# A fused attention, MLP and soft-MoE kernel: the denominator's reciprocal by way of DRAM instead of TensorE, K earlier, and the outputs' products in groups of four between second-layer products

## The chip, the cores and the metric

One NeuronCore of a Trainium2 chip runs the whole program. The time is device microseconds of one execution. Before the change three runs took 1055.14 to 1058.01 us, median 1057.03.

## What is computed

Inputs are q, k, v of 8 batches x 8 heads x 576 rows x 64, all fp32 (the weights w_in and w_out come as float64 words).

```python
def phi(x):                                  # 64 -> 128 -> 256 features
    proj = x @ w_phi
    proj = proj - max(abs(proj), axis=-1)
    return concat([exp(proj), exp(-proj)])
kv  = sum_s phi(k) v ;  z = sum_s phi(k)
x   = (phi(q) @ kv) / (phi(q) @ z + 1e-6)    # -> [4608, 512]
h   = x @ w_in                               # 512 -> 2048
g   = max(h, 0) + alpha * min(h, 0)
x   = g @ w_out                              # 2048 -> 512
logits = x @ phi                             # 512 -> 32 slots
d   = softmax(logits, over the 4608 tokens)
slot_input = d.T @ x                         # 32 x 512, 4 slots for each of 8 experts
slot_out[e] = max(slot_input[e] @ w1[e], 0) @ w2[e]
c   = softmax(logits, over the 32 slots)
out = c @ slot_out                           # [4608, 512]
```

## The kernel before, in words

Tokens go in 12 blocks of 384 (n = 0 to 11), the 2048 columns of w_in in 16 chunks (c). A pair (n, c) is a *slot* of the program; everything is registered for a slot with `at`, and a scheduler then sets each engine's order by slot and readiness. After the slots of blocks 4 and 7 stand five extra *virtual* steps each, in which two deferred blocks (0 and 1), whose g went to DRAM, are read back and finished. w_out is folded with phi at the start, so that g gives logits directly; x after w_out is never formed for all tokens, only the 32 sums over tokens (`pS`).

- `k_pair` (32 of them, one per batch and head pair): K's features (`pk`, `kp`), then kv and z (`pkv`, `pt`, `kv_t`, `zt`). `q_pair` (4 per block): load `qraw`, product `pq`, GpSimd's reduction, `qe`, then numerators `num` (L435) and denominators `den` (L442).
- `q_finish` (L453 on): ACT adds 1e-6 (`rd`), TensorE sums the two signs (`densum`, L460), DVE takes the reciprocal (L464), ACT and DVE split it into two float32r halves (`rhl`), TensorE spreads each head's row over 64 partitions by a selecting matrix (`sel`, L477 and L478, two products per p, eight per block), DVE multiplies the numerators by it (L484), ACT and DVE split x into `xhi` and `xlo`.
- `gemm` (L505): twelve float32r products of 128x128 by 128x384 per slot into `ph` (two banks); `leaky` makes g (`gT`); `turn_g` transposes it into `gb` and forms logits `pl` every fourth chunk; `softmax` keeps a running maximum, and `gather` and `add` accumulate `pS` into `acc`.
- The weights w1 and w2 and a copy of the folded w_out come in 144 pieces of 256 KB, prefetched into every buffer that falls free (`fetch`), 100 of them before the tail's own work, 44 when their buffers have been read (L686).
- Tail, after the last `gemm`: last softmax and `pS`, `pg`/`px` (slot sums times w_out), `psi`, `pe` (first layer), `pth` (TensorE transposes of h), `pso` (second layer, L819), `prp`, then `po` (L836): the outputs, each half of 256 columns in 36 products, copied by ACT and DVE into one of three 512 KB buffers `os` and written by 18 DMAs (L842). `pc` are transposes of the combine weights. `spin` issues products on an identity that nobody reads, so that TensorE stays busy.

SP issues every DMA, in its own order: a DMA that waits for its buffer holds up those behind it.

Of the kernel before, what the change touches and what calls it, by code (L numbers as in the profile page):

```python
# [28 lines left out]
TB = BT // 128  # L29
NT = T // 128  # L30
E = 8
# [3 lines left out]
KVB = 6  # L35
# [8 lines left out]
SPIN = [5, 3, 13, 6]  # L44

F64_LEAST = struct.unpack("<f", struct.pack("<I", 0x38100000))[0]
# [15 lines left out]
def attention_prelu_softmoe(ctx: ExitStack, tc, qT, kT, v, wphi, w_in, w_out, alpha, phi, w1, w2, out):  # L62
# [10 lines left out]
    gT_d = dram.tile([NDEF, NC, 128, BT], F32, name="gT_d")  # L73

# [27 lines left out]
    def spin(count, before):  # L102
        turn = bank("spin", ps_d)
# [28 lines left out]
    eps_den = const.tile([128, 1], F32, name="eps_den")  # L132
    densum = att.tile([128, 128], F32, name="densum")
    densel = xp.tile([128, NP, 128], F32R, tag="densel", name="densel")

    wpr = sm.tile([128, NC, NSL], F32, tag="wpr", name="wpr")
    acc = const.tile([128, 4, 512], F32, name="acc")
# [5 lines left out]
    def setup_a():  # L143
        nc.vector.memset(ones, 1.0)
        nc.vector.memset(eps_den, 0.0)
        nc.vector.memset(eps_den[0:32], 1e-6)
        nc.vector.memset(eps_den[64:96], 1e-6)

    def setup_b():
# [8 lines left out]
        for p in range(NP):  # L158
            for j in range(2):
                a, b = 64 * j + p, 64 * j + 32 + p  # L160
                r = 32 * p + 16 * j
                nc.vector.tensor_tensor(
                    out=densum[:, r:r + 16], in0=ident[:, a:a + 1].to_broadcast([128, 16]),
                    in1=ident[:, b:b + 1].to_broadcast([128, 16]), op=ALU.add)
                nc.vector.tensor_copy(densel[:, p, 64 * j:64 * j + 64], ident[:, r:r + 1].to_broadcast([128, 64]))

    sched = {}

# [14 lines left out]
    def conv(slot, src, use):  # L183
# [21 lines left out]
        def second():  # L205
# [3 lines left out]
            nc.vector.tensor_tensor(out=w, in0=m, in1=st["sign"], op=ALU.mult)  # L209
# [172 lines left out]
    def q_pair(slot, n, p, late=0):  # L382
# [44 lines left out]
        def attend():  # L427
# [25 lines left out]
    def q_finish(slot, n):  # L453
        st = q_st[n]

        def sums():
            rd = st["rd"] = sm.tile([128, BT], F32, tag="dT", name="rd")
            nc.scalar.activation(rd, st["den"][:, 0:BT], AF.Identity, bias=eps_den)
            ps = st["ps"] = bank("densum")
            nc.tensor.matmul(ps[:, 0:BT], densum, rd, start=True, stop=True)  # L460
# [28 lines left out]
        at(slot, "pe", sums)  # L489
        at(slot, "post", recip)  # L490
        at(slot + 1, "pre", split)
        for p in range(NP):
            at(slot + 1, "post", spread(p))
            at(slot + 1, "post", scale(p))
# [15 lines left out]
    def leaky(n, c, h):  # L510
        gT = gT_t[n, c] = sm.tile([128, 512], F32, tag="gT", name="gT", bufs=5)[:, 0:BT]
        if n < NDEF or (c % 2 == 0 and n < NB - 1):
            nc.scalar.activation(gT, h, AF.Relu, scale=-1.0)  # L513
            nc.scalar.activation(h, h, AF.Relu)  # L514
            nc.vector.scalar_tensor_tensor(out=gT, in0=gT, scalar=alpha_neg[:, c:c + 1], in1=h, op0=ALU.mult, op1=ALU.add)  # L515
        else:
            nc.vector.tensor_scalar(out=gT, in0=h, scalar1=0.0, scalar2=alpha_sb[:, c:c + 1], op0=ALU.min, op1=ALU.mult)  # L517
            nc.vector.scalar_tensor_tensor(out=gT, in0=h, scalar=0.0, in1=gT, op0=ALU.max, op1=ALU.add)
# [3 lines left out]
    def reload(n, c):  # L522
        gT4 = attk.tile([128, 4, BT], F32, tag=f"vg{c // 4 % 2}", name="gT4")
# [374 lines left out]
```

## Time and profile before

| | |
|---|---|
| median of three runs | 1057.03 us (1055.14 to 1058.01) |
| the profiled execution's own time | 1057.16 us |
| its span, first to last instruction | 1055.4 us |
| TensorE busy | 984.1 us (93%), mean granted clock 0.964 of full |
| DVE, ACT busy | 773.8 us (73%), 469.8 us (45%) |
| moved by DMA | 110.6 MB |

The profile has one line per group of instructions: engine, line of the kernel, result<-operands, shape, count, busy time, mean of one, and the idle time of that engine ahead of them with what ended it. A window view gives each engine's busy time in a stretch, with the granted TensorE clock (1.00 is 2.4 GHz, 0.5 is 1.2 GHz) and the DMA engines' share.

### The profile page before, as it was taken

The page shows a single profiled execution, that of the slowest core. Times are in us where ns is not written, and L with a number is a line of the kernel's source. Part 1 is how long each engine was busy: PE and PEld are TensorE (multiplying, and loading weights), DVE is VectorE, ACT ScalarE, POOL GpSimd, SP SyncE. Part 2 cuts the span into 40 slices and gives each one's busy share as a digit, 9 for nine tenths or more (in the row PEclk, how much of TensorE's full clock was granted, in tenths as well). Part 3 has the DMA queues.
Part 4 walks back from the last instruction along what each step waited for, and adds up shares of the span by engine and source line. Part 5 has one row for each costly group of instructions (what it writes and reads, how often), then busy time and mean ns, then how long its engine had stood idle before and what let it go on. Part 6 is the DMA issues. An engine that isn't in the chain of part 4 may idle for free.

```text
span 1055.4 us, 21864 instructions
## 1 busy us (share of the span) xinstructions
PE 984.1 (93%) x9038; PEld 685.2 (65%) x9038; DVE 773.8 (73%) x1552; ACT 469.8 (45%) x908; POOL 149.2 (14%) x88
## 2 busy tenths in 40 slices
PE   3787998998999999999999999999999999998994
PEld 1445776774676776676666776767667767787353
DVE  3999989879767578587878687687888486874133
ACT  3876867776444245144235344343334343200133
POOL 2201214121111212121112111121112221000000
PEclk7898999998999999999999999999999999999995
DMA  5343653653010111010401111110401200769879
GB/s 199 120 141 125 193 188 114 225 178 100 9 31 31 39 31 38 20 51 19 163 10 38 32 39 31 31 38 19 160 19 46 96 8 2 249 226 327 261 235 309
DMA packets 71986, 110.60 MB, mean 105 GB/s; under 512 B 7248, under 2 KB 47312, under 8 KB 71888
## 3 DMA queue, kind: packets, MB, share of 16 engines
q1 hardware_dynamic: 71888, 109.22, 32.0%
q8 instruction: 71, 1.16, 0.4%
q14 instruction: 27, 0.22, 0.1%
HBM read 89.27 MB, written 19.92 MB: 103 GB/s over the span
## 4 chain that ended last, share of the span: by engine, by line
PE 71%; DVE 3%; DMA 2%; ACT 1%; issue 1%; DVEq 0%; ACTq 0%; SPq 0%
PE ph L505 34%; PE num L435 5%; PE pS L602 5%; PE pkv L333 5%; PE pl L540 4%; PE den L442 3%; PE pq L403 3%; PE pk L289 2%; DMA out_dram<-os 2%; PE pso L819 1%; PE pe L782 1%; PE sel L477 1%; PE pt L355 1%; PE pr L558 1%; PE densum L460 1%; PE pkv L339 1%
## 5 line engine op out<-in xcount | busy, mean ns | idle before, releaser
L505 PE MATMUL ph<-xhi,w 128*128 128x384 f32 x1536 | 435.2, 351 | 6.5 <-DVE gT L515 4.4
L505 PEld LDWEIGHTS ph<-xhi,w 128*128 128x128 f32 x1536 | 279.0, 189 | 76.8 <-issue 41.5
L505 PE MATMUL ph<-xlo,w 128*128 128x384 f32 x768 | 255.1, 340 | 0.0
L415 POOL PARTITION_ALL_REDUCE mb<-pj x48 | 140.4, 2928 | 553.0 <-ACT pj L409 450.1
L505 PEld LDWEIGHTS ph<-xlo,w 128*128 128x128 f32 x768 | 143.6, 188 | 12.6 <-issue 6.1
L515 DVE SCALAR_TENSOR_TENSOR gT<-gT,alpha_neg,ph 128x384 f32<-128x384 f32 x104 | 62.9, 605 | 77.3 <-ACT ph L514 76.5
L532 DVE STREAM_TRANSPOSE gb<-gT 128x384 f32<-128x384 f32 x192 | 105.6, 566 | 5.7 <-DMA gT<-gT_d 1.9
L513 ACT ACTIVATE gT<-ph 128x384 f32<-128x384 f32 x104 | 50.8, 489 | 114.8 <-PE ph L505 114.0
L425 ACT ACTIVATE qe<-pj 128x768 f32<-128x768 f32 x92 | 73.9, 839 | 59.5 <-DVE pj L419 56.2
L517 DVE TENSOR_SCALAR gT<-ph,alpha_sb 128x384 f32<-128x384 f32 x88 | 53.8, 613 | 46.2 <-PE ph L505 45.8
L333 PE MATMUL pkv<-kp,vt 128*64 128x256 f32 (+1 forms) x640 | 85.0, 400 | 1.1 <-DVE wpr L250 1.1
L435 PE MATMUL num<-qe,kv 128*64 128x192 f32 (+1 forms) x496 | 70.9, 417 | 0.0
L283 ACT ACTIVATE kp<-kp 128x512 f32<-128x512 f32 (+1 forms) x80 | 46.8, 586 | 51.6 <-DVE kp L282 51.1
L333 PEld LDWEIGHTS pkv<-kp,vt 128*64 128x64 f32 (+1 forms) x640 | 41.3, 140 | 39.4 <-issue 17.1
L280 DVE TENSOR_REDUCE mx<-pk 128x4 f32<-128x512 f32 (+1 forms) x80 | 50.2, 627 | 11.4 <-PE pk L289 9.7
L602 PE MATMUL pS<-gb,d 32*32 32x256 f32 x2304 | 55.0, 385 | 0.3 <-DVE logits L594 0.2
L403 PE MATMUL pq<-qraw,wp 64*128 64x384 f32 x192 | 48.9, 562 | 6.7 <-DMA qraw<-in_qT_dram 4.1
L446 ACT COPY num<-num 128x384 f32<-128x384 f32 x48 | 22.8, 475 | 67.1 <-PE num L435 64.2
L409 ACT COPY pj<-pq 128x768 f32<-128x768 f32 x44 | 35.2, 799 | 36.3 <-PE pq L403 36.3
L419 DVE TENSOR_TENSOR pj<-pj,mb 128x768 f32<-128x768 f32 x48 | 46.6, 971 | 6.0 <-POOL mb L415 6.0
L282 DVE TENSOR_TENSOR kp<-pk,mx 128x512 f32<-128x512 f32 (+1 forms) x80 | 50.2, 627 | 0.8 <-PE pkv L333 0.2
L514 ACT ACTIVATE ph<-ph 128x384 f32<-128x384 f32 x104 | 50.6, 487 | 0.0
(191 smaller groups left out, 1345.6 us busy)
## 6 DMA issues: line engine op xcount, KB each, us to landing
w<-in_w_dram SPq DMA_DIRECT2D x58, 256.0 KB, 5.7
qraw<-in_qT_dram SPq DMA_DIRECT2D x48, 192.0 KB, 2.4
out_dram<-os SPq DMA_DIRECT2D x18, 512.0 KB, 3.7
raw<-in_w_in_dram SPq DMA_DIRECT2D x16, 512.0 KB, 3.6
raw<-in_w_out_dram SPq DMA_DIRECT2D x16, 512.0 KB, 4.2
gT_d<-gT SPq DMA_DIRECT2D x32, 192.0 KB, 2.0
gT<-gT_d SPq DMA_DIRECT2D x8, 768.0 KB, 5.2
pf<-in_w_dram SPq DMA_DIRECT2D x21, 256.0 KB, 6.0
```

Source lines behind the costliest of these rows:

```text
L333: return lambda: nc.tensor.matmul(pkv[64 * j:64 * j + 64, 0:256], vt[:, 64 * j:64 * j + 64], feats(t, j).rearrange("p s f -> p (s f)"), st ...
L403: lambda j=j, sl=slice(64 * j, 64 * j + 64): nc.tensor.matmul(pq[j][:, 0:BT], wp[sl], st["qraw"][sl], start=True, stop=True)
L415: nc.gpsimd.partition_all_reduce(mb, pj, 128, bass_isa.ReduceOp.absmax)
L425: nc.scalar.activation(st["e", s], pj, AF.Exp, scale=(1.0, -1.0)[s])
L435: lambda s=s, j=j: nc.tensor.matmul(num[64 * j:64 * j + 64, o:o + w], kvs[:, s, 64 * j:64 * j + 64], st["e", s][:, j, o:o + w], start=(s = ...
L505: gemm_last[0] = nc.tensor.matmul(h, (w_in_hi, w_in_lo)[a][c][:, 128 * k:128 * k + 128], (xhi, xlo)[b][:, k, :], start=(i == 0), stop=(i = ...
L513: nc.scalar.activation(gT, h, AF.Relu, scale=-1.0)
L514: nc.scalar.activation(h, h, AF.Relu)
L515: nc.vector.scalar_tensor_tensor(out=gT, in0=gT, scalar=alpha_neg[:, c:c + 1], in1=h, op0=ALU.mult, op1=ALU.add)
L517: nc.vector.tensor_scalar(out=gT, in0=h, scalar1=0.0, scalar2=alpha_sb[:, c:c + 1], op0=ALU.min, op1=ALU.mult)
L532: nc.vector.transpose(out=gb[n, c // 8][:, c % 8, :], in_=gT)
L602: lambda j=j, i=i, h=h: nc.tensor.matmul(pS[i][32 * (j % 4):32 * (j % 4) + 32, 256 * h:256 * h + 256], st["d"][32 * i:32 * i + 32, 32 * j: ...
```

## The change

1. **Reciprocal.** `den` is accumulated for both signs and both halves of a block's tokens in four column groups, so it needs no sum and holds 192 columns. DVE adds 1e-6 and takes the reciprocal of 128x192, SP writes it to DRAM (`rc_d`, two DMAs), and reads it back broadcast over 64 partitions (`bc`, two DMAs). Six slots on, DVE multiplies the numerators by it from SBUF (`divide`, held behind that slot's last marked DVE instruction). The set-up of the summing and selecting matrices, `rd` on ACT, `densum`, `rhl` and `sel` are gone. `q_finish` stands at slot 16(n-1)+7 (was +11), the multiplications at +13 (was +12).
2. **K.** Pairs 8 and on come up to eight slots sooner, with eight kv buffers (six); `q_pair`s stand three slots apart (four).
3. **Read-back of g** in tiles of two chunks: three buffers of two and the ring of `gT`, instead of two buffers of four.
4. **Tail.** `acc` in four tiles; for the last block TensorE adds the old sums (`carry`) and the copies are shared by ACT and DVE; first-layer results are masked and transposed by DVE (no `pth`); w2 pieces take rows 64 KiB apart for the partitions, in runs of 1 KB (2 KB apart before); combine weights stay transposed, so an output group is four products on 32 rows each (L859), without `pc`. Second-layer groups of the second half stand between the first nine output groups, with `spin`. Nine `os` buffers (three).

```diff
-SPIN = [5, 3, 13, 6]
+SPIN = [5, 3, 8, 3, 8, 5, 5, 5, 3]
...
-            for b, o, w in segments(n):
-                kvs, zt = kv_t[NP * b + p]
+            for s in (1, 0):
                 together([
-                    lambda g=g: nc.tensor.matmul(
-                        den[32 * g:32 * g + 32, o:o + w], zt[:, g, :], st["e", g % 2][:, g // 2, o:o + w],
-                        start=(p == 0 and o == 0), stop=(p == NP - 1 and o + w == BT))
-                    for g in (3, 1, 2, 0)])
+                    lambda j=j, h=h, zt=kv_t[NP * ((n * BT + h * HB) // S) + p][1]: nc.tensor.matmul(
+                        den[64 * j + 32 * h:64 * j + 32 * h + 32, 0:HB], zt[:, 2 * j + s, :],
+                        st["e", s][:, j, HB * h:HB * h + HB],
+                        start=(p == 0 and s == 1), stop=(p == NP - 1 and s == 0))
+                    for j in (1, 0) for h in (1, 0)])
...
         def recip():
-            rc = st["rc"] = sm.tile([128, BT], F32, tag="dT", name="rc")
-            nc.vector.reciprocal(out=rc, in_=st["ps"][:, 0:BT])
...
+            nc.vector.tensor_scalar(out=rd, in0=st["den"][:, 0:HB], scalar1=1e-6, scalar2=None, op0=ALU.add)
+            nc.vector.reciprocal(out=rd, in_=rd)
+            for j in range(2):
+                nc.sync.dma_start(rc_d[n % 2][j].rearrange("p h t -> h p t"), rd[64 * j:64 * j + 64])
+        def widen():
+            bc = st["bc"] = xp.tile([128, NP, BT], F32, tag="bc", name="bc")
+            for j in range(2):
+                nc.sync.dma_start(
+                    bc[64 * j:64 * j + 64], rc_d[n % 2][j, 0:NP].rearrange("p h t -> p (h t)").unsqueeze(0).to_broadcast([64, NP, BT]))
...
+                ins = nc.vector.tensor_tensor(out=xs, in0=st["bc"][:, p, :], in1=xs, op=ALU.mult).ins
+                tc.add_manual_dep(ins, mark[max(k for k in mark if k <= slot + 6)].name, nosync, reason="behind the load")
...
+        at(slot + 1, "pre", widen)
         for p in range(NP):
-            at(slot + 1, "post", spread(p))
-            at(slot + 1, "post", scale(p))
+            at(slot + 6, "post", divide(p))
+        for p in range(NP):
+            at(slot + 6, "post", scale(p))
...
-        k_pair(int(-40 + 2.5 * i) if i < 4 else int(-20 + 6 * (i - 4)) if i < 8 else 6 * i + -42, i)
+        k_pair(int(-40 + 2.5 * i) if i < 4 else int(-20 + 6 * (i - 4)) if i < 8 else 6 * i - 42 - min(i - 8, 8), i)
...
-                src = w2[e, 256 * c:256 * c + 256, 256 * dh:256 * dh + 256].rearrange("(c p) d -> p c d", p=128)
+                src = w2[4 * eg:4 * eg + 4].rearrange("e (f b) d -> (e f) b d", b=32)[:, 2 * b:2 * b + 2, 256 * dh:256 * dh + 256]
...
+            before = together([
+                lambda r=r, sl=slice(32 * r, 32 * r + 32): nc.tensor.matmul(
+                    po[r][:, 0:256], logits[sl, 4 * i:4 * i + 4, :].rearrange("p t s -> p (t s)"), sor[sl], start=True, stop=True)
+                for r in range(4)], before)
+            if dh == 0 and i < 7:
+                before = together(layer2(1, 9 + i), before)
+            before = spin(1 if dh == 0 else 2, before, idle)
+            for r in range(4):
+                (nc.vector.tensor_copy if r % 2 else nc.scalar.copy)(os_[:, r], po[r][:, 0:256])
```

TensorE at the turn from block 5 to block 6, before the change (w_1268 is chunk 15, w_637 chunk 0):

```order
L289 MATMUL pk<-wp,kraw 128x128 x8
L505 MATMUL ph<-xhi,w_1268 128x384
L477 MATMUL sel<-rhl,densel 128x384 x2
L478 MATMUL sel<-rhl,densel 128x384 x2
L477 MATMUL sel<-rhl,densel 128x384
L478 MATMUL sel<-rhl,densel 128x384
L442 MATMUL den<-qe,zt 32x192 x8
L477 MATMUL sel<-rhl,densel 128x384
L478 MATMUL sel<-rhl,densel 128x384
L505 MATMUL ph<-xhi,w_637 128x384 x4
L540 MATMUL pl<-gT,wpr 32x384 x4
```

and after it (w_1259 is chunk 15, w_633 chunk 0):

```order
L492 MATMUL ph<-xhi,w_1259 128x384 x2
L492 MATMUL ph<-xlo,w_1259 128x384
L492 MATMUL ph<-xhi,w_1259 128x384
L393 MATMUL pq<-qraw,wp 128x384 x2
L323 MATMUL pkv<-kp,vt 64x256 x10
L492 MATMUL ph<-xhi,w_633 128x384 x8
L492 MATMUL ph<-xlo,w_633 128x384
L393 MATMUL pq<-qraw,wp 128x384 x2
```

The eight `sel` products that stood ahead of and between chunk 0's first are gone.

SP after the change, around the reciprocal of block 4:

```order
L381 DMA qraw_3994<-in_qT_dram 128x384
L259 DMA kraw_4195<-in_kT_dram 128x512
L381 DMA qraw_4070<-in_qT_dram 128x384
L451 DMA rc_d0_74<-rd_4020 2x32x192 x2
L456 DMA bc_4026<-rc_d0_74 64x1536 x2
L259 DMA kraw_4460<-in_kT_dram 128x640
L381 DMA qraw_4162<-in_qT_dram 128x384
```

The four new DMAs stand behind loads of Q and K that wait for their buffers, and ahead of others.

TensorE in the tail, before:

```order
L819 MATMUL pso<-w_10248,hTm 32x256 x4
L819 MATMUL pso<-w_10251,hTm 32x256 x4
L819 MATMUL pso<-w_10254,hTm 32x256 x4
L836 MATMUL po<-sor,cT 128x256 x36
L825 MATMUL prp<-so,tident 128x256
L836 MATMUL po<-sor,cT 128x256 x36
```

and after:

```order
L823 MATMUL pso<-w_10220,acc_111 32x256 x4
L823 MATMUL pso<-w_10223,acc_112 32x256 x4
L859 MATMUL po<-sor,logits 128x256 x4
L823 MATMUL pso<-w_10226,acc_112 32x256 x4
L108 MATMUL idle<-ident 128x128
L859 MATMUL po<-sor,logits 128x256 x4
L823 MATMUL pso<-w_10229,acc_112 32x256 x4
```

The second half's second-layer products, all ahead of the outputs before, now stand one group of four behind each of the first seven output groups.

## Rows read from the trace of the kernel before

**Rows 1.** The page, busy time of each engine over the span.
```profile
PE 984.1 (93%) x9038; PEld 685.2 (65%) x9038; DVE 773.8 (73%) x1552; ACT 469.8 (45%) x908; POOL 149.2 (14%) x88
```
**Rows 2.** Windows: stretch, busy us (count) per engine, clock, DMA share, GB/s.
```profile
80.00:90.00 10.00, 4.66 (x12) 3.47 (x13) 10.00 (x20) 6.08 (x13) 0.00 (x0) 0.56 0.15 52
90.00:165.00 75.00, 72.73 (x623) 55.15 (x621) 68.26 (x119) 53.12 (x104) 16.25 (x9) 0.97 0.56 183
395.10:471.80 76.70, 76.70 (x659) 51.62 (x658) 57.95 (x110) 32.83 (x62) 13.86 (x9) 1.00 0.13 37
625.20:701.90 76.70, 76.70 (x659) 51.62 (x658) 57.95 (x110) 32.83 (x62) 13.86 (x9) 1.00 0.12 37
```
**Rows 3.** Groups by line: busy us, mean ns, idle before and its releaser.
```profile
L477 PE MATMUL sel<-rhl,densel 128*128 128x384 f32 x48 | 18.2, 401 | 8.0 <-DVE num L484 5.6 <-ACT rhl L469 2.4
L464 DVE RECIPROCAL rc<-densum 128x384 f32<-128x384 f32 x12 | 30.7, 2557 | 21.7 <-PE densum L460 21.7
L280 DVE TENSOR_REDUCE mx<-pk 128x4 f32<-128x512 f32 (+1 forms) x80 | 50.2, 627 | 11.4 <-PE pk L289 9.7
```
**Rows 4.** Timeline of TensorE, blocks 4 to 5: start us, us, instructions.
```profile
459.66 0.91 PE L460 MATMUL densum<-rd,densum 128*128 128x384 f32 x2
460.50 2.53 PE L333 MATMUL pkv<-kp,vt 128*64 128x256 f32 x20
...
469.44 0.85 PE L442 MATMUL den<-qe,zt 128*32 128x384 f32 x8
...
473.60 0.45 PE L477 MATMUL sel<-rhl,densel 128*128 128x384 f32 x1
473.88 0.34 PE L478 MATMUL sel<-rhl,densel 128*128 128x384 f32 x1
...
474.40 0.86 PE L505 MATMUL ph<-xhi,w 128*128 128x384 f32 x4
```
**Rows 5.** Timeline of TensorE: the same denominators in pieces of 192 columns.
```profile
309.20 0.86 PE L442 MATMUL den<-qe,zt 128*32 128x192 f32 x16
```
**Rows 6.** Waits of TensorE: us in total, times, longest.
```profile
PE sel L477 <- DVE num L484: 5.6, 3, 1.9
PE sel L477 <- ACT rhl L469: 2.4, 1, 2.4
PE sel L478 <- DVE rhl L470: 1.9, 3, 1.3
```
**Rows 7.** The page, DMA issues: count, KB each, median us to landing.
```profile
gT_d<-gT SPq DMA_DIRECT2D x32, 192.0 KB, 2.0
gT<-gT_d SPq DMA_DIRECT2D x8, 768.0 KB, 5.2
```
**Rows 8.** Waits of SP's queue.
```profile
SPq L391 <- PE pq L403: 224.4, 33, 22.3
```
**Rows 9.** The chain that ended last, in the tail: start us, us.
```profile
948.05 6.48 PE ph L505 x36
...
976.30 5.02 PE px L762 x32
...
995.72 4.41 PE pe L782 x34
```
**Rows 10.** Timeline of SP in the tail: first issue, us to the last one's end.
```profile
964.10 9.16 SPq L686 DMA_DIRECT2D gb<-in_w_dram  x12
...
1024.25 26.85 SPq L842 DMA_DIRECT2D out_dram<-os  x18
```
**Rows 11.** Windows in the tail, columns as in rows 2.
```profile
1000.00:1010.00 10.00, 10.00 (x135) 5.64 (x134) 3.44 (x23) 2.67 (x5) 0.00 (x0) 1.00 1.10 349
...
1040.00:1050.00 10.00, 5.62 (x24) 4.30 (x23) 4.16 (x7) 3.24 (x7) 0.00 (x0) 0.67 1.02 340
```
**Rows 12.** Groups by line in the tail, columns as in rows 3.
```profile
L836 PE MATMUL po<-sor,cT 128*128 128x256 f32 x72 | 15.8, 372 | 8.6 <-ACT os L841 7.0 <-DVE sor L830 1.6
...
L841 ACT COPY os<-po 128x512 f32<-128x512 f32 x18 | 10.5, 587 | 18.9 <-DMA out_dram<-os 12.5 <-PE po L836 6.3
```

More of the change, by code (lines that the diff above doesn't have):

```diff
@@ L29 @@
 TB = BT // 128
+HB = BT // 2
 NT = T // 128
@@ L34 @@
 VT = 5
-KVB = 6
+KVB = 8
 PF = 14
@@ L100, in together, with spin @@
         return before
-    def spin(count, before):
-        turn = bank("spin", ps_d)
+    def spin(count, before, turn=None):
+        turn = turn or bank("spin", ps_d)
         return together([
@@ L157, in setup_b @@
             nc.vector.tensor_tensor(out=o, in0=o, in1=ident[:, 96:128], op=ALU.add)
[L158 to L165, printed above, removed]
     sched = {}
+    mark = {}
     after = [NC * (b + 1) + VR for b in VB]
@@ L546, in attention_prelu_softmoe @@
     first = [True]
-    gemm_last, spun = [None], [None]
+    gemm_last, spun, last = [None], [None], {}
     def softmax(step, n):
@@ L600, in gather @@
             pS = st["pS"] = [bank("pS"), bank("pS"), two[:, 0], two[:, 1]]
-            last = together([
+            end = together([
                 lambda j=j, i=i, h=h: nc.tensor.matmul(
@@ L606, in gather @@
             if n == NB - 1:
-                spun[0] = spin(SPIN[3], last)
+                spun[0] = spin(SPIN[4], end)
         def add():
@@ L772, in attention_prelu_softmoe @@
-    hTm = [attk.tile([128, 4, E, NSL], F32, tag="kp2", name="hTm", bufs=KPB) for f in range(2)]
-    for t in hTm:
-        nc.gpsimd.memset(t, 0.0)
-    hrs = attk.tile([128, 2, 512], F32, tag="kp2", name="hrs", bufs=KPB)
-    hr_t = {}
-    for eg in range(2):
+    pa = last["pa"]
+    spun[0] = spin(SPIN[5], together([
+        lambda i=i: nc.tensor.matmul(pa[32 * i:32 * i + 32, :], tident[:, 0:32], acc[i], start=False, stop=True)
+        for i in range(4)], spun[0]))
+    half = [slice(0, 256), slice(256, 512)]
@@ new lines, in attention_prelu_softmoe @@
+    nc.scalar.copy(acc[0][:, half[0]], pa[:, half[0]])
+    nc.vector.tensor_copy(acc[1][:, half[1]], pa[:, half[1]])
+    pg, px, psi = bank("pg"), bank("px"), bank("psi")
+    spun[0] = spin(SPIN[6], together([
+        lambda c=c: nc.tensor.transpose(pg[:, 128 * c:128 * c + 128], acc[c // 2][:, 128 * c:128 * c + 128], ident)
+        for c in range(4)], spun[0]))
+    nc.scalar.copy(aT[:, half[0]], pg[:, half[0]])
+    nc.vector.tensor_copy(aT[:, half[1]], pg[:, half[1]])
+    spun[0] = spin(SPIN[7], together([
+        lambda i=i, c=c: nc.tensor.matmul(
+            px[32 * c:32 * c + 32, :], aT[:, 128 * c + 32 * i:128 * c + 32 * i + 32], got["wo", 4 * i + c], start=(i == 0), stop=(i == 3))
+        for i in range(4) for c in range(4)], spun[0]))
@@ new lines, in attention_prelu_softmoe @@
+    nc.scalar.activation(acc[2][:, half[0]], px[:, half[0]], AF.Identity, scale=lsum)
+    nc.vector.tensor_scalar(out=acc[3][:, half[1]], in0=px[:, half[1]], scalar1=lsum, scalar2=None, op0=ALU.mult)
+    for k in range(KD):
+        nc.tensor.matmul(psi[:, 32 * k:32 * k + 32], acc[2 + k // 2][:, 128 * k:128 * k + 128], tident[:, 0:32], start=True, stop=True)
+    nc.scalar.copy(sT, psi[:, 0:KD * NSL].rearrange("p (k s) -> p k s", k=KD))
+    own = sm.tile([128, 8], F32, tag="sc", name="own", bufs=2)
@@ new lines, in attention_prelu_softmoe @@
+    for eg in range(2):
+        for j in range(4):
+            nc.vector.tensor_reduce(
+                out=own[:, j:j + 1], in_=ident[:, 36 * j + 16 * eg:36 * j + 16 * eg + 4], axis=AX.X, op=ALU.add)
+        nc.vector.tensor_reduce(out=own[:, 4 + eg:5 + eg], in_=own[:, 0:4], axis=AX.X, op=ALU.add)
+    nc.vector.tensor_scalar(out=own[:, 4:6], in0=own[:, 4:6], scalar1=F32_MOST, scalar2=None, op0=ALU.mult)
+    hT = []
+    for eg in range(2):
+        hr = attk.tile([128, EF], F32, tag="kp2", name="hr", bufs=KPB)
@@ L822, in attention_prelu_softmoe, with layer2, slots_out @@
+    def layer2(dh, m):
+        eg, b0 = divmod(4 * m, 32)
+        return [
+            lambda b=b: nc.tensor.matmul(
+                pso[dh][32 * (b % 4):32 * (b % 4) + 32, :], hT[eg][b // 16][:, 32 * (b % 16):32 * (b % 16) + 32],
+                got["w2", dh, eg, b // 2][:, b % 2, :], start=(eg == 0 and b < 4), stop=(eg == 1 and b >= 28))
+            for b in range(b0, b0 + 4)]
+    def slots_out(dh):
         so = so2[:, dh, :]
-        nc.vector.tensor_copy(so, pso)
+        nc.vector.tensor_copy(so, pso[dh])
```

232 lines of the change are left out of this document (104 added, 128 removed).

## The prediction

> **What bounds the kernel now.** I read the page's busy times first: TensorE works 984.1 of 1055.4 us [rows 1]. An average hides stages, so the windows come next. Between 395 and 702 us a block takes 76.7 us: the two stretches 230.1 us apart agree to the digit, three blocks lie between them, and TensorE has no idle time in either while DVE is busy 57.95 of 76.70 [rows 2]. There, a microsecond taken from TensorE's products is a microsecond of the span. At the start it is otherwise: from 80 to 90 us DVE is busy 10.00 of 10 and TensorE 4.66 at a clock of 0.56, and from 90 to 165 us both are nearly full, 68.26 and 72.73 of 75 [rows 2]. There DVE binds as much. Last, the tail: the last chunk's product ends at 948.05 + 6.48 = 954.5 (call it G) [rows 9], and 100.9 us follow it. The weights' loads run at 349 GB/s while TensorE is busy 10 of 10, and the outputs at 340 GB/s while it is busy 5.6 of 10 [rows 11]: in the tail two stages stand one behind the other, TensorE's and then the outputs' DMA (18 issues from 1024.25 on, over 26.85 us [rows 10]).
>
> The sum is made against the profiled execution, 1057.16 us with a span of 1055.4, so 1.8 us lie around the span; it stands 0.1 us above the median of the runs.
>
> **Reciprocal: taken from TensorE.** Four `sel` products after a change of shape take from 473.60 to 474.40, 0.80 us; the pair for `densum` takes from 459.66 to 460.50, 0.84 [rows 4]. Eight `sel` in two fours and one `densum` are 2.44 us a block; where `sel` stands between like products, with no change of shape, it costs (474.40 − 473.88)/3 = 0.173, so 8 x 0.173 + 0.84 = 2.23. In 12 blocks 26.7 to 29.3; I take **−28**. `sel` was also waited for, 5.6 + 2.4 + 1.9 = **−9.9** us of idle TensorE [rows 6]; the idle of 7 us ahead of the weight loads is the same time seen by another unit and isn't counted again. The denominators change from 8 products of 384 columns to 16 of 192: 0.85 and 0.86 us in the rows [rows 4, 5], so nothing. Some of the waits let the clock fall: 4.66 us busy at 0.56 would be 2.6 at full clock, 2 saved [rows 2], and the two later waits of `sel` on DVE have such a stretch each; I take **−3**, between 0 and −5.
>
> **Reciprocal: put in its place.** The way is now: add and reciprocal on DVE, write, broadcast read, multiplication. The reciprocal has half the columns, so half of 2557 ns [rows 3]. The write is nearest to a 192 KB write of g, 2.0 us, and the read, 128 partitions by 6 KB, to a read of 768 KB, 5.2 us [rows 7]. With 0.4 for the added pass (an estimate, a sixth of the reciprocal) that is 1.7 + 2.0 + 5.2 = 8.9 us. The multiplication stands six slots on, 6 x 76.7/16 = 28.8 us. So in the full blocks the trip is hidden with 20 us to spare, and the cover gone would cost up to 8.9 us a block. Block 0 is the exception: there, in the changed order, 15 DVE instructions lie between reciprocal and multiplication; at 10.00 us for 20 [rows 2] that is 7.5 us against the trip's 7.2, a wait of 0 to 3. The multiplications and splits of x now fall close to the block's turn, where TensorE needs `xhi` at once: +1, between 0 and 4.
>
> **K sooner.** Over the whole kernel its work is the same. In blocks 0 and 1 one more of the 32 pairs has to be done, by the slot numbers (5i − 34 in place of 6i − 42). Two of its DVE passes, the reduction and the subtraction like it, take 2 x 50.2/32 = 3.1 us a pair [rows 3], and sums and copies come on top; against them stand 1.3 us of each reciprocal and the set-up that is gone. TensorE had only 2.3 us of slack in the 75 [rows 2], DVE 6.7. I take +3, bounds 0 and 12 (these two passes four times over, none of it hidden). With block 0's wait of 1 and the turn's 1 the new waits are **+5**, in all 0 to +19. `q_pair`'s spacing moves products among full slots: nothing.
>
> **Read-back of g.** Two deferred blocks read by twos rather than fours. A 768 KB read lands in 5.2 us [rows 7], a smaller one sooner, and each is issued a virtual step ahead: nothing. Were a step's cover gone, one trip for each of two blocks would come to the path, up to +10.
>
> Body: −28 − 9.9 − 3 + 5 = **−36**.
>
> **Tail.** If DMA never rests, its work sets the end. The first round's last load is issued at 964.10 + 9.16 = 973.3 [rows 10] and lands like a 768 KB read at most 5.2 later [rows 7], 978.5 or G + 24. Then 46 pieces of 256 KB at 349 GB/s are 46 x 0.751 = 34.5, to G + 58.5, and 18 outputs of 512 KB at 340 GB/s are 18 x 1.54 = 27.8 [rows 11], to G + 86.3; one more for the last landing, G + 87.3. Before it was G + 100.9: **−13.5**. This asks that outputs are ready by G + 58.5 and then keep up. `pe` ended at 995.72 + 4.41 = 1000.1, G + 45.6 [rows 9], and should end some 5 sooner, since the sums' DVE additions and the copies ahead of `px` (which ended at G + 26.8 [rows 9]) are split. The first half's 64 second-layer products, each like a product of the same 256 columns, take at most 64 x 0.372/4 = 6, in fours as before, so the first output group stands near G + 50. For the pace, a group's four output products cost between 0.37 together and 1.49 one after the other (372 ns each [rows 12]); with a second-layer group of 0.37 and a spin of less, 0.9 to 2.1 us against 1.54 of DMA. I take the lower half, as the four fill different rows, and the queue of loads until G + 58.5 gives 8 us of lead. The copies are two of half size on each engine, at most 2 x 0.587 [rows 12], below 1.54. The three buffers before cost ACT 12.5 us of waiting for outputs [rows 12]; with nine that wait goes, and the DMA's own pace is late next.
>
> One row speaks against the interleaving: the first `sel` after products of another shape takes 0.28 us to the next, later ones 0.173 [rows 4], 0.1 for each change. The Trainium skill, "TensorEngine Tiling (Array Packing)", section "Tiling Modes", says why one would expect that: changing the tiling mode drains the engine. By it each of nine groups would pay three changes, 3 x 0.1 x 9 = 3 us, and the sum would lose that only if TensorE set the pace; with DMA setting it nothing is lost.
>
> Sum: 1057.2 − 36 − 13.5 = 1007.7, **1008 us**.
>
> **The rivals.**
>
> *DVE takes over at the start.* For it: 10.00 of 10 busy, and a pair more. Against: 6.7 us of room from 90 us on. It costs up to 12 in place of 3, and up to 5 of the waits of `sel` come back: 1015 to 1022.
>
> *The tail gains nothing.* w2's rows now lie 64 KiB apart from partition to partition, and no transfer in these rows is laid out so; or the four products run one after the other. Without the 13.5 it is 1021; with loads slowed by a third, 46 x 0.25 = 11.5 more, 1033; 1019 to 1036 in all. The Trainium skill, "DMA: Bandwidth & Descriptors", section "Latency and other measured facts", has copies slow down at large power-of-two row pitches in HBM: 207 GB/s at 512 KiB where 214 is full, 103 at 4 MiB. By its mildest figure, 3%, the 46 loads would lose an estimated 1 us; no row of before has such a pitch.
>
> *Slower than before.* SP issues in order, and the four new DMAs stand behind loads of Q and K. SP has waited up to 22.3 us for a `qraw` buffer [rows 8]. The multiplication stops DVE in order behind it, so g stops, and TensorE runs dry once both `ph` banks are full, one slot (4.8) later. The cover is 28.8 + 4.8 − 8.9 = 24.7 us; at 11 turns each microsecond above it costs 11. From (36 + 13.5)/11 = 4.5 above, a delay of 29.2 us, nothing is left of the gain; at 31 it is 1008 + 11 x 6.3 = 1077. Against it: the longest single wait is 22.3, and the loads were ordered by need.
>
> *No change.* What TensorE no longer does turns up as idle time at the turns, since `xhi` comes as late as before, and the tail's outputs still wait: 1055 to 1059.
>
> *Faster still.* None of the new waits: 1003; and K and first loads sooner bring the first round's end 5 earlier: 996 to 998.
>
> **How the numbers follow.** The forecast has 0.64, with a range of its own of 999 to 1015 (the new waits from 0 to +12); DVE at the start 0.12, the tail without gain 0.12, faster still 0.06, no change 0.02, slower 0.04. Faster by over 0.3% (3 us, what a measurement of this kernel can tell) is 0.64 + 0.12 + 0.12 + 0.06 = 0.94. The range of 994 to 1030 leaves out slower, no change, the upper part of the tail's failure and a little below: about 0.14.
>
> **What would show it.** Right: no waits of TensorE at the turns, a block of 74.3 to 74.5 us in the middle, outputs issued from about G + 51 with the DMA share near 1 from G + 24 to the end, and a tail of 87 us. Wrong: waits of TensorE for `xhi` or for g behind `num` at each turn (SP late), more than 8 us of idle TensorE between 80 and 165 us (DVE), loads of w2 at well under 349 GB/s or gaps in DMA between G + 58 and the end (tail).

## The result, and the profile after

The changed kernel takes 1012.5 us (median of four, 1010.69 to 1013.46); the kernel before took 1057.5 beside it. The ratio is 0.957, with a 95% interval of 0.954 to 0.960. Forecast were 1008, between 994 and 1030. The profiled execution took 1010.69 us, with a span of 1008.9: 46.5 us less than before's span, where 49.5 were forecast.

The page gives the busy time of each engine over the span; TensorE's is 34.7 us less than in [rows 1]:

```profile
PE 949.4 (94%) x9266; PEld 666.9 (66%) x9266; DVE 761.1 (75%) x1509; ACT 446.1 (44%) x883; POOL 145.1 (14%) x86
```

To see where the span went, I cut both at the first and behind the last product of `gemm`. Windows of the kernel before (columns as in [rows 2]), start, body and tail:

```profile
0.00:88.90 88.90, 56.52 (x529) 31.21 (x530) 71.31 (x159) 57.92 (x106) 13.36 (x16) 0.82 0.43 143
88.90:954.50 865.60, 846.58 (x7672) 606.10 (x7672) 670.25 (x1293) 388.73 (x753) 133.92 (x70) 0.99 0.25 80
954.50:1055.40 100.90, 80.95 (x841) 47.92 (x839) 32.19 (x101) 23.14 (x50) 1.90 (x2) 0.86 0.86 280
```

and of the changed kernel:

```profile
0.00:87.80 87.80, 59.68 (x612) 33.48 (x612) 66.15 (x136) 55.45 (x101) 13.65 (x18) 0.92 0.50 158
87.80:923.00 835.20, 813.53 (x7729) 589.24 (x7726) 663.30 (x1290) 373.62 (x733) 131.41 (x68) 0.99 0.32 94
923.00:1008.90 85.90, 76.19 (x933) 44.13 (x931) 31.64 (x84) 16.99 (x49) 0.00 (x0) 0.97 1.02 336
```

The tail gave 15.0 us (forecast 13.5), start and body 31.5 (forecast 36). In the body TensorE works 33.1 us less, but its idle time, stretch less busy, grew from 19.0 to 21.7. Where that idle time lies, two windows show, the first to be held against the second line of [rows 2], and of TensorE's waits the one that is new (us in total, times, longest):

```profile
90.00:165.00 75.00, 64.39 (x549) 49.11 (x548) 64.53 (x116) 53.41 (x105) 15.88 (x9) 0.98 0.60 184
...
394.80:467.00 72.20, 72.03 (x671) 49.13 (x667) 54.29 (x103) 31.04 (x59) 14.31 (x8) 1.00 0.18 48
```

```profile
PE ph L492 <- ACT xhi L465: 7.0, 2, 6.4
```

In the middle TensorE is full, as before. The second window is block 4 alone, and blocks differ among themselves, since K pairs and virtual steps don't fall evenly. Three blocks, from block 5's first product to block 8's, take 74.4 us each, for 76.7 [rows 2] (74.3 to 74.5 was forecast):

```profile
467.00:690.20 223.20, 221.55 (x2245) 152.50 (x2241) 173.79 (x344) 89.04 (x173) 34.91 (x20) 1.00 0.21 59
```

From 90 to 165 us TensorE is idle for 10.6 us instead of 2.3, and 6.4 of them are one wait: block 1's first product for its `xhi`. DVE's timeline there:

```profile
152.69 1.35 DVE L449 RECIPROCAL rd<-rd 128x192 f32<-128x192 f32 x1
153.96 0.62 DVE L316 TENSOR_TENSOR ks<-ks,kp 64x512 f32<-64x512 f32 x1
157.69 0.61 DVE L502 SCALAR_TENSOR_TENSOR gT<-gT,alpha_neg,ph 128x384 f32<-128x384 f32 x1 [3.11 <-ACT ph L501]
164.33 1.97 DVE L472 TENSOR_TENSOR num<-bc,num 128x384 f32<-128x384 f32 x4 [6.03 <-DMA bc<-rc_d]
```

and SP's:

```profile
154.07 1.12 SPq L451 DMA_DIRECT2D rc_d<-rd  x2
156.99 0.50 SPq L456 DMA_DIRECT2D bc<-rc_d  x1
157.58 0.53 SPq L381 DMA_DIRECT2D qraw<-in_qT_dram  x1
158.21 0.48 SPq L456 DMA_DIRECT2D bc<-rc_d  x1
```

The reciprocal of block 1 ends at 154.0 and its copy lands at 164.3: a trip of 10.3 us. Its cover, what DVE has to do meanwhile, is two instructions, and SP issues a load of Q between the two halves of the read. The stretch behind it runs in part at the lower clock, 0.57 on average:

```profile
160.00:172.00 12.00, 6.51 (x29) 5.70 (x30) 7.67 (x16) 5.38 (x11) 0.00 (x0) 0.57 0.43 115
```

Over all blocks the multiplication waits 9.1 us for the trip, in blocks 0 (3.1) and 1 (6.0) alone; in the ten others it is hidden:

```profile
L472 DVE TENSOR_TENSOR num<-bc,num 128x384 f32<-128x384 f32 x48 | 23.6, 554 | 9.1 <-DMA bc<-rc_d 9.1
```

In the tail the DMA engines are busy from 923 to 1003 us, where [rows 11] had loads and outputs in separate stretches:

```profile
923.00:933.00 10.00, 7.79 (x90) 5.41 (x89) 6.71 (x31) 1.55 (x5) 0.00 (x0) 1.00 0.91 287
...
963.00:973.00 10.00, 10.00 (x176) 6.86 (x168) 3.55 (x6) 0.00 (x0) 0.00 (x0) 1.00 1.10 350
973.00:983.00 10.00, 10.00 (x124) 4.70 (x122) 3.12 (x8) 3.19 (x10) 0.00 (x0) 1.00 1.09 352
983.00:993.00 10.00, 9.54 (x92) 5.21 (x84) 4.99 (x13) 4.48 (x15) 0.00 (x0) 1.00 1.08 382
993.00:1003.00 10.00, 10.00 (x85) 6.56 (x85) 5.91 (x15) 5.00 (x16) 0.00 (x0) 1.00 1.03 355
```

SP issues the last load at 977.15 and the first output at 977.92, one behind the other:

```profile
977.15 0.37 SPq L702 DMA_DIRECT2D xlo<-in_w_dram  x1
977.92 26.05 SPq L867 DMA_DIRECT2D out_dram<-os  x18
```

TensorE's timeline of one output group, four products (recorded as eight), four of the second layer and one that nobody reads:

```profile
977.13 0.71 PE L859 MATMUL po<-sor,logits 32*128 32x256 f32 x8
977.77 0.64 PE L823 MATMUL pso<-w,acc 128*32 128x256 f32 x8
978.34 0.49 PE L108 MATMUL idle<-ident 128*128 128x128 f32 x2
978.76 0.71 PE L859 MATMUL po<-sor,logits 32*128 32x256 f32 x8
```

A group takes 1.63 us, changes of shape included; from the first group to the last of the eighteen, 975.50 to 1001.61, it is 1.54 a group. Ahead of the first stand the first layer (`pe`) and 200 records, that is 100 products, of the second (`pso`), back to back, as the chain that ended last shows:

```profile
949.66 13.94 PE pe L805 x128
963.60 9.06 PE pso L823 x166
...
973.29 2.28 PE pso L823 x34
```

### The profile page after: what moved, and what is told of

The parts are those of the page before. It is cut to its first block, busy times and chain, and to the rows that moved or that the text cites. A ratio compares the mean times of both kernels' runs of the same rounds, so it can differ in the third digit from the quotient of the medians.

```text
span 1008.9 us, 22365 instructions
## 1 busy us (share of the span) xinstructions
PE 949.4 (94%) x9266; PEld 666.9 (66%) x9266; DVE 761.1 (75%) x1509; ACT 446.1 (44%) x883; POOL 145.1 (14%) x86
## 4 chain that ended last, share of the span: by engine, by line
PE 68%; DVE 6%; DMA 1%; ACT 1%; issue 1%; SPq 0%; DVEq 0%; ACTq 0%
PE ph L492 34%; PE num L425 5%; PE pkv L323 5%; PE pS L596 4%; PE pl L533 3%; PE pq L393 3%; PE den L431 3%; PE pk L279 2%; PE pso L823 2%; PE pe L805 1%; PE po L859 1%; PE idle L108 1%; DVE gb L525 1%; PE pr L551 1%; PE pt L345 1%; PE spin L108 1%
## 5 line engine op out<-in xcount | busy, mean ns | idle before, releaser
L279 PE MATMUL pk<-wp,kraw 64*128 64x128 f32 x512 | 39.7, 298 | 14.0 <-issue 10.0
L425 PEld LDWEIGHTS num<-qe,kv 128*64 128x64 f32 x496 | 31.8, 136 | 28.9 <-issue 18.1
```

The source lines that it names most:

```text
L279: lambda t=t, j=j, sl=slice(64 * j, 64 * j + 64): nc.tensor.matmul(st["pk"][:, j, F * t:F * t + F], st["kraw"][sl, 128 * t:128 * t + 128], ...
L425: lambda s=s, j=j: nc.tensor.matmul(num[64 * j:64 * j + 64, o:o + w], kvs[:, s, 64 * j:64 * j + 64], st["e", s][:, j, o:o + w], start=(s = ...
```

## The experiments

Theory A was: the body's gain is what TensorE no longer does and no longer waits for, and it fell short because block 1's trip is not covered; the tail's end is set by DMA. All ratios are to the kernel before on the same chip.

**Part 1 undone (e2_sel).** The old denominators, `densum`, `sel` and `q_finish` in the changed kernel.

```diff
-            nc.vector.tensor_scalar(out=rd, in0=st["den"][:, 0:HB], scalar1=1e-6, scalar2=None, op0=ALU.add)
-            nc.vector.reciprocal(out=rd, in_=rd)
...
+            nc.tensor.matmul(ps[:, 0:BT], densum, rd, start=True, stop=True)
...
+                nc.tensor.matmul(ps[:, 0:BT], densel[:, p, :], st["rhi"], start=True, stop=False)
+                nc.tensor.matmul(ps[:, 0:BT], densel[:, p, :], st["rlo"], start=False, stop=True)
...
-        q_finish(-39 + 18 + 5 if n == 0 else NC * (n - 1) + 7, n)
+        q_finish(-39 + 18 + 5 if n == 0 else NC * (n - 1) + 11 - (n == 1), n)
```

> The changed kernel with the reciprocal's way alone put back as it was (denominators by segments, densum, sel, q_finish at slot 16(n-1)+11); K, read-back and tail stay changed. Theory A, that TensorE's work and the waits of sel were the body's gain: +28 for products, +8 to +10 for waits, less the 6.4 us stall that the changed kernel has at the turn from block 0 to 1 and some 3 of its clock, so 1012.5 + 27 to + 32 = 1037 to 1045. Rival, that the earlier K pairs gave most of the body's gain: 1013 to 1025.

Measured: 1063.1 us, ratio 1.006 (1.004 to 1.007): slower than before, though it keeps the new tail. Both expectations were too low. Windows of its body, and of a stretch in block 1:

```profile
89.00:972.50 883.50, 860.36 (x7672) 608.33 (x7672) 677.77 (x1286) 384.98 (x753) 135.06 (x68) 0.98 0.25 78
```

```profile
241.00:269.00 28.00, 24.38 (x142) 15.05 (x143) 25.13 (x50) 15.62 (x34) 6.09 (x2) 0.63 0.39 112
```

The body is 48.3 us longer than the changed kernel's, and 17.9 longer than that of before with the same 7672 records of products. TensorE is busy 13.8 us longer for them and idle 4.1 us longer. In the stretch shown, 24.38 us at a clock of 0.63 would be 15.4 at full clock, so 9.0 are lost to the clock; but the body before had such stretches too. An estimate over the whole body (busy time times the share of the clock that was not granted, in steps of 0.1 us) gives 14.2 lost here and 7.7 before, so the clock has 6.5 of the 13.8, and the other 7.3 stay open. So what is left of the change doesn't suit the old way of the reciprocal: start and body are 49.5 us longer than the changed kernel's, where all parts together had gained 31.5. Whether it is K's places, Q's or g's read-back that doesn't suit it, this run doesn't tell. It does say that the earlier K pairs alone did not give the gain.

**K pairs late again (e1_k_late).**

```diff
-        k_pair(int(-40 + 2.5 * i) if i < 4 else int(-20 + 6 * (i - 4)) if i < 8 else 6 * i - 42 - min(i - 8, 8), i)
+        k_pair(int(-40 + 2.5 * i) if i < 4 else int(-20 + 6 * (i - 4)) if i < 8 else 6 * i - 42, i)
```

> The changed kernel with K pairs 8 and on back at slots 6i - 42, everything else changed. Theory A, that the earlier pairs are only what the earlier reciprocal asks for and cost little: without them the denominators of the blocks in which a batch begins come late and the trip shows at those turns, DVE waiting for bc in three to seven blocks, 1017 to 1035 (ratio 0.962 to 0.979). Rival, that the pairs merely crowd DVE in blocks 0 and 1: 1005 to 1012 (0.950 to 0.957).

Measured: 1023.0 us, ratio 0.967 (0.965 to 0.969), within theory A's bounds. Its body, and the waits of the multiplication (us, times):

```profile
88.00:933.40 845.40, 814.13 (x7729) 592.14 (x7726) 659.69 (x1290) 374.53 (x733) 131.72 (x68) 0.99 0.31 93
```

```profile
  DMA bc<-rc_d: 16.7, 4
```

TensorE's work is that of the changed kernel, its idle time is 31.3 us for 21.7, and the trip shows in four blocks for two. So the earlier K pairs hide the trip; they are worth some 10 us. Nor do they crowd anything that shows: from the first product of block 0 to that of block 3 it is 237.7 us here, and 239.7 and 237.9 in the two profiles of the changed kernel (after, c0_same). And even so the body is 20.2 us shorter than before's.

**No trip in block 1 (e6_no_trip1).** Block 1 is multiplied by block 0's reciprocals, so its own are not used.

```diff
-            for j in range(2):
+            for j in range(0 if n == 1 else 2):
...
         def widen():
+            if n == 1:
+                st["bc"] = q_st[0]["bc"]
+                return
```

> The changed kernel without the way through DRAM in block 1 alone: its numerators are multiplied by block 0's reciprocals, which are in SBUF already; everything else is unchanged. Theory A, that block 1's trip (10.3 us from the reciprocal's end to its landing, two DVE instructions of cover) costs the 4.5 us by which the body fell short: the 6.4 us gap ahead of block 1's first product and most of the stretch at half clock go, 1003 to 1007. Rival, that DVE's own backlog of the first 150 us bounds that turn, so that the wait only moves: 1010 to 1013.

Measured: 1001.4 us, ratio 0.947 (0.946 to 0.949), beyond theory A's lower bound.

```profile
87.80:913.40 825.60, 812.84 (x7729) 587.80 (x7726) 664.29 (x1291) 373.00 (x733) 128.51 (x68) 1.00 0.31 94
```

The same work, 12.8 us idle for 21.7: the body is 9.6 us shorter (6.5 against c0_same, whose body took 832.1). So what block 1's multiplication waits for costs more than the 4.5 us by which start and body fell short. By itself this run does not split it, since here the multiplication waits for no denominators either; m1_sel1 below does.

**Batch 1's K pairs sooner (e7_k47).** A way to have those denominators earlier.

```diff
-        k_pair(int(-40 + 2.5 * i) if i < 4 else int(-20 + 6 * (i - 4)) if i < 8 else 6 * i - 42 - min(i - 8, 8), i)
+        k_pair(int(-40 + 2.5 * i) if i < 4 else int(-20 + 5 * (i - 4)) if i < 8 else 6 * i - 42 - min(i - 8, 8), i)
```

> The changed kernel with K pairs 5, 6 and 7 (batch 1) one, two and three slots sooner; nothing else. The last denominators of block 1 then stand behind chunk 12 of block 0 on TensorE, where the changed kernel has them behind chunk 14. Theory A, that the stall at the turn to block 1 is the trip's 10.3 us against what is left of block 0 after those denominators: two chunks more of cover, some 9 us, so the 6.4 us gap and the stretch at half clock go: ratio to before 0.946 to 0.951 (1000 to 1006). Rival, that DVE's backlog moves the wait elsewhere: 0.954 to 0.960 as now.

Measured: 1015.0 us, ratio 0.959 (0.957 to 0.962): the rival. Block 1's last denominators, and the multiplication:

```profile
152.76 0.53 PE L431 MATMUL den<-qe,zt 128*32 128x192 f32 x8
```

```profile
164.49 1.96 DVE L472 TENSOR_TENSOR num<-bc,num 128x384 f32<-128x384 f32 x4 [5.57 <-DMA bc<-rc_d]
```

In the order they stand two chunks earlier, in time they are later than in the changed kernel (there the last ones start at 149.9). From 135.0 to 152.0 DVE is busy 16.5 of 17.0 us and TensorE 16.8: where both are full, what comes sooner in the order pushes other work behind it. More of block 0 now stands behind the denominators, but the multiplication still stops DVE for 5.6 us, and TensorE then waits 5.1 us for ACT ahead of block 1. With w_out's conversions put off by three slots in addition (e8_k47_conv) it was 1020.3 us, ratio 0.964 (0.963 to 0.966), where less was expected:

> As e7_k47, and w_out's conversions three slots later at first and one slot apart (13 + c in place of 10 + 1.25c), so that DVE has less to do in block 0. Theory A, that what is left at the start is DVE: 2 to 5 us below e7_k47. Rival, that with block 1's stall gone nothing binds there: within 2 us of e7_k47.

Neither of these two orders of DVE's work helped. The second loses its time in block 2: from that block's first product to the next block's it is 94.5 us for 86.7 in e7_k47, with 5.5 us of idle TensorE for 2.3; why was not followed.

**Block 1 by TensorE (m1_sel1), beside the changed kernel again (c0_same).** Sixteen products of an identity's column, repeated, spread block 1's reciprocals; no DRAM.

```diff
-            for j in range(2):
+            for j in range(0 if n == 1 else 2):
...
+                        lambda j=j: nc.tensor.matmul(
+                            ps[64 * j:64 * j + 64, HB * h:HB * h + HB],
+                            ident[:, 64 * j + 32 * h + p:64 * j + 32 * h + p + 1].to_broadcast([128, 64]), st["rd"], start=True, stop=True)
...
+        if n == 1:
+            for p in range(NP):
+                at(slot + 1, "post", spread(p))
+                at(slot + 1, "post", scale(p))
+            return
```

> The changed kernel as it is, on the chip of the two runs beside it, so that these can be read against it: 0.954 to 0.960 of before.

> The changed kernel, but block 1's reciprocals are spread by TensorE instead of by DRAM: sixteen fp32 products of a column of the identity, repeated 64 times, by 192 tokens, two to a PSUM half; the multiplication reads PSUM. All other blocks go through DRAM. The output stays the reference's. Theory A, that the trip of block 1 is what stalls the turn: the products cost 2 to 4 us, the 6.4 us gap, the half clock and DVE's wait of 6 us go: 0.945 to 0.951 of before, 6 to 12 us under the changed kernel beside it. Rival, that e6_no_trip1 gained because it did not wait for the denominators either: 0.954 to 0.958, with a gap of TensorE at that turn still over 4 us.

Measured: c0_same 1010.0 us, ratio 0.955 (0.953 to 0.957); m1_sel1 1008.8, 0.954 (0.951 to 0.956). No difference is clear. The products at the turn:

```profile
154.92 1.52 PE L465 MATMUL sel<-rd,ident 128*64 128x192 f32 x16 [0.19 <-DVE rd L449]
...
157.46 0.87 PE L465 MATMUL sel<-rd,ident 128*64 128x192 f32 x8
158.26 0.79 PE L511 MATMUL ph<-xhi,w 128*128 128x384 f32 x3
```

The stall at the turn is gone, as theory A said: block 1's first product starts at 158.3, in c0_same at 166.0. These windows run from the first product of block 0 to that of block 3 and from there to the end of the body, first in m1_sel1, then in c0_same, then the first of them in e6_no_trip1:

```profile
88.00:322.50 234.50, 224.40 (x1857) 165.10 (x1853) 207.88 (x403) 158.00 (x312) 43.74 (x23) 1.00 0.46 139
322.50:920.90 598.40, 591.26 (x5908) 424.72 (x5905) 454.61 (x890) 216.24 (x422) 86.45 (x45) 1.00 0.25 75
```

```profile
89.50:327.40 237.90, 221.87 (x1825) 164.86 (x1821) 207.97 (x401) 157.16 (x312) 43.47 (x23) 0.99 0.46 141
327.40:921.60 594.20, 590.57 (x5908) 423.78 (x5905) 454.63 (x890) 216.25 (x422) 86.46 (x45) 1.00 0.26 76
```

```profile
87.80:319.10 231.30, 222.44 (x1826) 164.22 (x1822) 209.61 (x403) 156.79 (x312) 42.43 (x23) 0.99 0.46 141
```

In blocks 0 to 2 TensorE is idle for 16.0 us in c0_same, 10.1 in m1_sel1, which waits for the denominators but for no trip, and 8.9 in e6_no_trip1, which waits for neither. So, on one execution each, the trip has some 6 of these 7 us and late denominators about 1 (DVE's order around the multiplications differs a little in the two). m1_sel1 is not faster for two reasons. With the products of its own TensorE is busy 2.5 us longer in blocks 0 to 2. And 4.2 us are lost from block 3 on: block 8 takes 77.4 us for 74.7 and block 11 45.5 for 43.6. In block 8 one of TensorE's waits is new, for the read-back of g:

```profile
PE pl L552 <- DMA gT<-gT_d: 2.1, 1, 2.1
```

Moving block 9's reciprocal one slot later, so that SP issues those read-backs ahead of it (m3_fin9):

```diff
-        q_finish(-39 + 18 + 5 if n == 0 else NC * (n - 1) + 7, n)
+        q_finish(-39 + 18 + 5 if n == 0 else NC * (n - 1) + 7 + 1 * (n == 9), n)
```

> m1_sel1 with block 9's reciprocal one slot later (q_finish at 16(n-1)+8 for n = 9 alone), which puts the last three read-backs of g of the second deferred block ahead of that reciprocal's four DMAs on SP. m1_sel1 gained 4.9 us up to block 3 and lost 2.1 us of TensorE waiting for g's read-back at 724.9 us, with a stretch at half clock behind it. Theory A, that those read-backs came late because they stood behind the reciprocal's write and its landing on SP: that wait goes, 2 to 4 us under m1_sel1, 0.950 to 0.9525 of before. Rival, that the read-backs wait for their buffers: as m1_sel1, 0.952 to 0.956.

Measured: 1010.2 us, ratio 0.955 (0.952 to 0.957), the rival's number. The read-back's wait fell to 0.2 us, as theory A said, but DVE now waits for block 9's own trip; g behind it is late, and TensorE waits 3.1 us for that, in block 8 again:

```profile
748.74 1.97 DVE L486 TENSOR_TENSOR num<-bc,num 128x384 f32<-128x384 f32 x4 [2.78 <-DMA bc<-rc_d]
```

Block 0 by TensorE as well (m2_sel01) was slower, 1015.6 us, ratio 0.961 (0.958 to 0.963), the rival's side. The loss lies ahead of block 3, whose first product starts at 332.2 us for 322.5 in m1_sel1; it was not followed further:

> As m1_sel1, with block 0 by TensorE too. DVE waited 3.1 us for block 0's trip in the changed kernel, with DVE full before and after. Theory A, that at the start DVE's idle time is lost time: 1 to 4 us below m1_sel1. Rival, that TensorE's products and their half clock at 80 us cost as much: within 1.5 us of m1_sel1 or above it.

No version ran that is clearly faster than the changed kernel and computes the same.

**Three output buffers (e3_os3).**

```diff
-            os_ = wring.tile([128, 4, 256], F32, tag=f"w{7 + i}", name="os")
+            os_ = wring.tile([128, 4, 256], F32, tag=f"w{8 + i % 3}", name="os")
```

> The changed kernel with three output buffers in place of nine (the same prefetch). Theory A, that DMA alone sets the tail's end and is busy throughout: within 2 us of 1012.5. Rival, that the buffers matter because outputs' copies, waiting for a write behind the queue of loads, stop TensorE ahead of the second-layer groups: 1015 to 1022, with TensorE waiting for ACT or DVE copies between 976 and 1003.

Measured: 1017.7 us (1016.0 to 1025.1), ratio 0.964 (0.960 to 0.968): the rival. TensorE's wait for a copy, and the window behind it:

```profile
984.36 0.74 PE L859 MATMUL po<-sor,logits 32*128 32x256 f32 x4 [2.39 <-ACT os L866]
```

```profile
983.00:993.00 10.00, 8.64 (x59) 3.87 (x59) 3.54 (x9) 2.58 (x8) 0.00 (x0) 0.66 0.72 251
```

ACT's copy at 983.94 has waited 4.6 us for an output to land, TensorE waits for the copy, the clock falls to 0.66, and the DMA engines, which should set the end, are busy 0.72.

**Second layer first (e5_l2_first).**

```diff
-    for m in range(9):
+    for m in range(16):
         for call in layer2(1, m):
...
-            if dh == 0 and i < 7:
-                before = together(layer2(1, 9 + i), before)
```

> The changed kernel with all of the second half's second-layer products ahead of the outputs. They are 7 x 0.57 = 4.0 us of TensorE less between the first outputs. Theory A, that DMA sets the tail and the loads' queue covers the first outputs: within 2 us of 1012.5. Rival, that the first outputs come 4 us later behind loads that are done by then: 1014 to 1017, with a dip of the DMA share under 0.9 between 975 and 985 us.

Measured: 1017.8 us, ratio 0.963 (0.961 to 0.965), the rival's number by another way. TensorE's and SP's timelines, and the window between loads and outputs:

```profile
976.36 4.26 PE L823 MATMUL pso<-w,acc 128*32 128x256 f32 x24 [0.21 <-DMA w<-in_w_dram]
```

```profile
984.95 24.95 SPq L865 DMA_DIRECT2D out_dram<-os  x18
```

```profile
980.00:986.00 6.00, 5.70 (x44) 2.40 (x44) 1.62 (x5) 1.29 (x4) 0.00 (x0) 1.00 0.20 64
```

The outputs come 7 us later, not 4: all of them now stand behind products that need the last pieces of w2, so loads and outputs no longer overlap, and the DMA engines run dry between them for some 5 us (6.0 at a share of 0.20). Counted from G, which is 921.7 here, the first output comes 8.4 us later and the tail is 8.2 us longer, 94.1 for 85.9. The outputs also move more slowly, 340 GB/s between 993 and 1013 us where the changed kernel had 382 and 355; why was not followed.

**w2's rows as before (e4_w2rows).** The second layer's rows are then in another order than its first factor's.

```diff
-                src = w2[4 * eg:4 * eg + 4].rearrange("e (f b) d -> (e f) b d", b=32)[:, 2 * b:2 * b + 2, 256 * dh:256 * dh + 256]
+                src = w2[4 * eg + b // 4, 256 * (b % 4):256 * (b % 4) + 256, 256 * dh:256 * dh + 256].rearrange("(c p) d -> p c d", p=128)
```

> The changed kernel with w2's pieces read by the rows of before (2 KB from partition to partition rather than 64 KB); the second layer then multiplies by rows in another order. Theory A, that the pitch costs nothing: within 2 us of 1012.5, loads at some 350 GB/s as now. Rival, that the pitch of 64 KB slows the loads: 1001 to 1008, and over 360 GB/s between 963 and 973 us.

Measured: 1009.2 us, ratio 0.955 (0.953 to 0.957), that of c0_same and between the two ranges, so the rate has to decide. Loads run at the same rate as in the changed kernel, 348 and 350 GB/s:

```profile
963.00:973.00 10.00, 10.00 (x179) 6.73 (x172) 2.65 (x5) 0.37 (x1) 0.00 (x0) 1.00 1.10 348
```

So no cost of the 64 KB pitch shows.

## Why the prediction was right, and where it was off

The forecast of 1008 was 4.5 us low, and its range held. The sum had 1007.7. 1.8 us lie between the profiled execution and the median; the rest is a body that gave 4.5 less than the sum had and a tail that gave 1.5 more, so part of the nearness is luck.

- *Products and clock, −28 and −3.* TensorE's busy time fell by 33.1 us in the body and rose by 3.2 at the start, where K pairs now stand: 29.9 for 31. Right, and the split too: by the estimate used for e2_sel, the body before lost 7.7 us to the clock and the changed one's lost 3.1, so 28.5 of the 33.1 are products and 4.6 the clock.
- *Waits, −9.9 and +5.* Idle time fell by 4.3 us at the start and rose by 2.7 in the body: 1.6 less in place of 4.9. This is the step that failed. Of `sel`'s 9.9 us, 4.3 lay in the body, and 7.0 of waits for `xhi` came in their place. "In the full blocks the trip is hidden with 20 us to spare" was worked out from slot numbers, with block 0 as the one exception. Blocks 2 to 11 bear it out. Block 1 does not: its last denominators are done at 150.7, 6.0 us before block 0's last product ends, and the order of the changed program has two DVE instructions between its reciprocal and its multiplication, a count that the prediction made for block 0 alone. What it cost shows in m1_sel1: some 6 us of idle TensorE, nearly all of it the trip. The trip was also mis-sized, 10.3 us for 7.2: 2.9 from the write's issue to the read's, 1.2 until the second half of the read is issued, and 6.1 to its landing.
- *K sooner, +3.* The sign was wrong. I priced the crowding of DVE and not what the pairs are for; without them the trip shows in four blocks and it costs some 10 us, and blocks 0 to 2 get faster by at most 2 (e1_k_late).
- *Read-back, nothing.* Right in the changed kernel, where TensorE waits 0.3 us for it; m1_sel1, with 2.1, shows how little cover it has.
- *Tail, −13.5.* 15.0, by the mechanism forecast: DMA work from G to the end. Two things in it were luck. The first output was put at G + 50 and was issued at G + 54.9. The first layer ended at G + 40.6, as the sum had it; but 100 second-layer products stand ahead of the first group, not 64, and take 0.114 us each (11.4 us for 100), not 0.372/4 = 0.093. So of the lead of 8 us over the end of the loads some 3 were left, an estimate from e5_l2_first, where the DMA engines run dry some 3 us after the last load's issue. A delay of 8.4 us ahead of the first output cost 8.2 there, some 5 of it with DMA dry. And a group takes 1.63 us while second-layer products stand in it and 1.54 over all eighteen, the very pace of the DMA that was to hide it. So the tail is balanced between TensorE and DMA rather than bound by one: the DMA engines hardly rest, and the chain that ended last runs through TensorE.
- *A price misread.* The 372 ns of one product [rows 12] run from its start to its end, and products overlap: 72 of them kept TensorE busy for 15.8 us, 0.22 each. So "0.37 together and 1.49 one after the other" weren't the bounds that they were meant to be; the measured 0.64 lies between them all the same.
- *The rules weighed.* Changes of shape cost what the row had: four second-layer products take 0.57 us in a group (977.77 to 978.34) and 0.43 among their like (24 in 2.59 us from 964.69 on), 0.14 more for 0.1. That they cost the tail nothing isn't shown, with TensorE as busy as the DMA engines; from the first output on these stay at a share of 1.03 to 1.09. As for the pitch, "DMA: Bandwidth & Descriptors" of the Trainium skill ("Latency and other measured facts") lists 512 KiB as its lowest, with a small loss; at 64 KB the runs show none (e4_w2rows).
- *The rivals.* SP did not hold the writes up: block 1's is issued at 154.07, as the reciprocal ends. DVE at the start was the rival nearest to what happened, with its place right and its mechanism not: it was not one more K pair (e1_k_late), but the in-order multiplication that stopped a full engine.

Open: why e2_sel's TensorE is busy for 7.3 us more than the clock explains, and which of the other parts made it slower than before. Why m1_sel1 and m3_fin9 show a gap of 1.6 us in block 11 for which the profile names no releaser is open too.

## What to carry to other kernels

Read a cover in the order of the changed program, for the worst block and not the typical one, and ask what sets the time of its start: where an engine is full, slots say nothing about time. Edits that look separate can lean on each other: without the earlier K the way through DRAM loses 10 us of its gain, and the rest of the change without the way through DRAM makes the kernel slower than it was. In a tail where loads give way to stores, what counts is that stores can start before the loads end; nine buffers were worth 7 us of the tail (92.8 in e3_os3 for 85.9) and products placed between the outputs 8.

## What was not expected of the hardware

A reciprocal of 96 KB took 10.3 us through DRAM and back as 768 KB, at a DMA share of 0.55 (150 to 165 us), where the write and read rows of before gave 7.2 [rows 7]. Four fp32 products on 32 rows each take 0.64 us from the first one's start to the next group of another shape (977.13 to 977.77), 0.16 each. Before the change a product did the same share of the outputs on all 128 rows, in float32r, and at a granted clock of 1.00 it took about as long, 0.17 each:

```profile
1022.72 3.31 PE L836 MATMUL po<-sor,cT 128*128 128x256 f32 x20
```
